# Attention and channel MLP on one core: from coarse phases ordered by a scheduler to one written order of even steps

## The chip, the cores and the metric

The kernel runs on one core of one Trainium2 chip, as a single launch. Times are device microseconds (us) of whole executions. The kernel before took 446.32 us at the median of three runs (440.49 to 447.17). The experiments came in four sets, each on another chip, with runs of the kernel before in each. The record calls a run slow when it took over 1.5% longer than the fastest run of the same kernel in its set; ratios leave slow runs out, the medians given here do not.

The engines have the profile's names: PE (matrix engine; PEld is its weight load), DVE (vector engine), ACT (scalar engine), POOL and SP. POOL and SP also issue DMAs. PEclk is the clock granted to PE, as a share of full speed. PSUM is the memory into which PE writes its results; a ring is a set of buffers used in turn. The span is the time from the first to the last instruction of an execution.

## The reference, cut to what matters

```python
# attention: q, k, v of (8 batches, 8 heads, 576 tokens, 64), omega (128, 64)
def phi(x):
    proj = np.einsum('bhsd,md->bhsm', x, omega)
    return np.concatenate([np.cos(proj), np.sin(proj)], axis=-1) / np.sqrt(m)
q_p, k_p = (phi(q), phi(k))
kv = np.einsum('bhsm,bhsd->bhmd', k_p, v)
z = np.sum(k_p, axis=2)
num = np.einsum('bhsm,bhmd->bhsd', q_p, kv)
den = np.einsum('bhsm,bhm->bhs', q_p, z)
...                                    # attn = num / den; x = heads side by side
# mixer: x (8, 576, 512), U (576, 32), V (32, 576), w_ch1 (512, 2048), w_ch2 (2048, 512)
h = xt @ U @ V                         # xt: x with tokens last
u = x + h.transpose(0, 2, 1)
ch = np.maximum(u @ w_ch1, 0.0) @ w_ch2
return (u + ch).astype(np.float32)
```

Work comes in 32 pairs of heads, four pairs to a batch. Two pairs share one load of k, q and v (a "quad" of heads). When a batch's four pairs are done, its tokens are mixed (U and V), and then the two MLP layers, W1 with relu and W2, can run. One batch needs 64 matmuls of 512 columns for each layer, and the ninth token row ("tail") of two batches is done together.

## The kernel before

Comments with L numbers give the lines that the profile names. A pair's attention is a chain over four engines. PE makes projections (`pk`, `pt`, `pq`), DVE turns them into integer angles, ACT takes the sine, POOL shifts the same angles in place by a quarter turn, and ACT takes the sine again for the cosine:

```python
def sine(g, a):
    ang, ft = st[g]
    low = ...
    nc.scalar.activation(out=ft[:, 0, a, :], in_=low, func=ACT.Sin, scale=TO_RAD)      # L181
    nc.gpsimd.tensor_scalar(out=ang[:, a, :], in0=ang[:, a, :], scalar1=TURN / 4.0,
                            scalar2=1.0, op0=ALU.add, op1=ALU.mult)                      # L182
def cosine(g, a):
    ...
    nc.scalar.activation(out=ft[:, 1, a, :], in_=low, func=ACT.Sin, scale=TO_RAD)      # L188
```

`key_values` and `numerators` then use these features (`kv_ps`, `nd`), and DVE divides into `x`. POOL also issues the loads of k, q and v, and copies ("widens") v into tiles with a column of ones:

```python
def load(n, names):
    for name in names:
        raw[name, n] = rawp.tile([P, 2, NS * D], BF16, name=f"{name}raw")
        ordered(nc.gpsimd.dma_start(raw[name, n], quad(...)))                           # L146
def widen_v(n):
    ordered(nc.gpsimd.tensor_copy(vq[n % NV][:, :, 0:D], raw.pop(("v", n))...))         # L149
```

The MLP of one batch is four chunks, one for each step: eight tiles of W1, eight tiles of W1, two token tiles of W2, two token tiles of W2.

```python
def channel_in(b, fs):                       # hid has one buffer
    for f0 in fs[::2]:
        h_ps = psum.tile([P, 2, SM], F32, name="h_ps", tag="mm")
        for f in range(2):
            for ct in range(NCT):
                nc.tensor.matmul(h_ps[:, f, :], w1(ct, f0 + f), uT[:, :, ct, :], ...)   # L351
            nc.scalar.activation(out=hid[:, f0 + f, :], in_=h_ps[:, f, :], func=ACT.Relu)  # L353

for s in range(1, NG + 6):
    if s >= 6:
        b, mc = divmod(s - 6, 4)
        if b < B:
            mlp_chunk(b, mc)
    n = s // 2 + 1
    if s % 2 == 0 and 4 <= n < NG // 2:
        load(n, "kqv")
        transpose_quad(n)
        widen_v(n)                           # the v whose load was just issued
    if s < NG:
        angles(s)
    ...
    if s != 4:
        attend(s - 1)                        # key_values, numerators, and every fourth time the mix
```

The framework's scheduler then reorders the instructions of each engine, so the order that runs is not quite this one. PSUM has a ring of two double banks for attention and mixing ("at") and one for the MLP ("mm").

## Time and profile before

| | before |
|---|---|
| median time | 446.32 us |
| span of the profiled execution | 441.5 us |
| PE, ACT, DVE, POOL busy | 376.0, 227.7, 199.7, 133.3 us |
| two batches in the steady part (pair 15 to pair 23) | 103.5 us |

PE is busy for most of the span. These are lines of the page's parts 1 and 2 for the kernel before: busy us with the share of the span, then tenths of busy time and of the clock in 40 slices.

```profile
PE 376.0 (85%) x3675; PEld 191.3 (43%) x3675; DVE 199.7 (45%) x338; ACT 227.7 (52%) x280; POOL 133.3 (30%) x145
...
PE   3866886988899988988899988978899989979995
...
PEclk9968898999999998989999998998999999998999
```

Busy time overstates the work. The next lines are groups of the same kernel: count, busy us, mean ns of one; after the second bar, the engine's idle time before them and what ended it.

```profile
L351 PE MATMUL h_ps<-uT,W1b 128*128 128x512 bf16 x512 | 127.6, 391 | 25.5 <-ACT hid L353 23.7 <-ACT qT L166 0.9
L376 PE MATMUL ch_ps<-W2b,hid 128*128 128x512 bf16 x512 | 127.0, 392 | 3.9 <-DVE o L379 3.9
```

One such matmul shows 391 ns, but the ends are 216 ns apart at the median; near the end of the span, from 401.02 us on, 64 in a row took 13.89 us (217 ns each). From here on we measure lost PE time as spacings between matmul ends of more than 0.4 us. They add to 104.9 us in the kernel before; this overstates the loss, as each of the 132 spacings also contains the time of the matmul that ends it, 0.216 us at the median for 512 columns.

W1 matmuls wait 23.7 us for relu (`hid`), in the second field above. Why relu is late can be seen in the waits: engine and instruction, what it waited for, us in total, times, longest.

```profile
ACT hid L353 <- PE h_ps L351: 73.4, 62, 19.1
...
PE h_ps L351 <- ACT hid L353: 23.7, 22, 4.2
POOL vq_108 L149 <- DMA vraw<-in_v_dram: 18.9, 4, 7.5
...
POOL vq_112 L149 <- DMA vraw<-in_v_dram: 17.1, 3, 5.9
...
POOL vq_110 L149 <- DMA vraw<-in_v_dram: 9.0, 2, 5.7
...
POOL vq_114 L149 <- DMA vraw<-in_v_dram: 7.1, 1, 7.1
```

The four buffers of v make 52.1 us of waiting. One such place is in the timeline of the kernel before (start, us, engine, line, operation, and in brackets the idle time before it):

```profile
155.59 0.73 POOL L146 DMA_DIRECT2D vraw<-in_v_dram  x1
...
163.68 1.15 POOL L149 COPY vq_108<-vraw 128x1152 bf16<-128x1152 bf16 x1 [4.79 <-DMA vraw<-in_v_dram]
164.80 1.14 POOL L182 TENSOR_SCALAR ang<-ang 128x1152 int32<-128x1152 int32 x1
165.97 1.16 ACT L188 ACTIVATE ft<-ang 128x1152 bf16<-128x1152 int16 x1 [3.69 <-POOL ang L182]
167.04 1.06 ACT L353 ACTIVATE hid<-h_ps 128x512 bf16<-128x512 f32 x2
167.67 0.61 PE L351 MATMUL h_ps<-uT,W1b 128*128 128x512 bf16 x2 [3.19 <-ACT hid L353]
```

POOL waits for a load that it issued just before, and widens; then comes the angle shift, then ACT's cosine, then relu, then PE, which had a gap of 3.19 us. Of the W1 matmuls that follow, eight in a row are 410 to 428 ns apart instead of 216: half clock (the granted clock from 167.6 to 171.3 us is 0.57).

### The profile page before, as it was taken

Reading aid. Unit: us, or ns where it says so; the run is one execution under the profiler, and the core shown is the slowest. Engines: PE = TensorE matmul, PEld = TensorE weight load, DVE = VectorE, ACT = ScalarE, POOL = GpSimd, SP = SyncE. Lnnn points to the kernel's source line nnn. Section 1 sums busy time; section 2 is a strip of 40 time slices with the busy share of each in tenths; the row PEclk is TensorE's granted clock in tenths of the full one; section 3 lists DMA queues with packets and bytes.
Section 4 is the critical chain, followed back from the end, with each engine's and each line's share of the span. In section 5 each row is a group of like instructions: output and inputs, shape, how many; then the busy total and the mean of one; then the engine's idle time right before and its main releaser. Section 6 shows DMA issues by size and latency. Waiting matters only on the chain.

```text
span 441.5 us, 8568 instructions
## 1 busy us (share of the span) xinstructions
PE 376.0 (85%) x3675; PEld 191.3 (43%) x3675; DVE 199.7 (45%) x338; ACT 227.7 (52%) x280; POOL 133.3 (30%) x145
## 2 busy tenths in 40 slices
PE   3866886988899988988899988978899989979995
PEld 2553343434464433434456443434446444434452
DVE  2966451564436541664435551674343462460011
ACT  2975684327834465625755094635773277504420
POOL 5794435313323240523333052433332121200000
PEclk9968898999999998989999998998999999998999
DMA  8999294858073590585536473285809320133023
GB/s 137 173 152 199 46 176 70 137 114 144 16 123 61 119 135 1 94 150 99 83 48 136 90 117 49 30 157 108 134 3 181 73 49 0 25 62 70 1 48 72
DMA packets 71765, 40.64 MB, mean 92 GB/s; under 512 B 50608, under 2 KB 66992, under 8 KB 71728
## 3 DMA queue, kind: packets, MB, share of 16 engines
q0 software_dynamic: 17280, 18.35, 27.5%
q1 hardware_dynamic: 54448, 21.75, 24.9%
q8 instruction: 28, 0.46, 0.5%
q14 instruction: 9, 0.07, 0.1%
HBM read 37.14 MB, written 9.44 MB: 105 GB/s over the span
## 4 chain that ended last, share of the span: by engine, by line
PE 48%; ACT 13%; DMA 11%; POOL 10%; DVE 9%; issue 8%; POOLq 0%; ACTq 0%; DVEq 0%
PE ch_ps L376 23%; PE h_ps L351 11%; DMA vraw<-in_v_dram 8%; POOL ang L182 5%; ACT ft L181 5%; DVE ang L172 5%; ACT ft L188 4%; DMA qraw<-in_q_dram 4%; PE ch_ps L388 3%; PE ht_ps L364 3%; ACT hid L353 3%; PE nd L266 2%; DVE u L325 2%; ACT hidt L366 1%; POOL kraw L146 1%
## 5 line engine op out<-in xcount | busy, mean ns | idle before, releaser
L351 PE MATMUL h_ps<-uT,W1b 128*128 128x512 bf16 x512 | 127.6, 391 | 25.5 <-ACT hid L353 23.7
L376 PE MATMUL ch_ps<-W2b,hid 128*128 128x512 bf16 x512 | 127.0, 392 | 3.9 <-DVE o L379 3.9
L182 POOL TENSOR_SCALAR ang<-ang 128x1152 int32<-128x1152 int32 x64 | 73.5, 1149 | 177.0 <-ACT ft L181 176.4
L353 ACT ACTIVATE hid<-h_ps 128x512 bf16<-128x512 f32 x128 | 73.2, 592 | 73.6 <-PE h_ps L351 73.4
L188 ACT ACTIVATE ft<-ang 128x1152 bf16<-128x1152 int16 x64 | 74.0, 1159 | 46.0 <-POOL ang L182 45.5
L181 ACT ACTIVATE ft<-ang 128x1152 bf16<-128x1152 int16 x64 | 73.9, 1160 | 39.4 <-DVE ang L172 36.5
L351 PEld LDWEIGHTS <-W1b 128*128 128x128 bf16 x512 | 48.2, 99 | 78.3 <-issue 32.6
L376 PEld LDWEIGHTS <-hid 128*128 128x128 bf16 x512 | 48.0, 100 | 61.2 <-issue 14.0
L379 DVE TENSOR_TENSOR o<-ch_ps,u 128x512 f32<-128x512 f32 x32 | 22.1, 690 | 85.2 <-PE ch_ps L376 84.9
L172 DVE TENSOR_SCALAR ang<-pk 128x1024 int32<-128x1024 f32 x32 | 39.0, 1220 | 39.9 <-PE pt L211 34.8
L172 DVE TENSOR_SCALAR ang<-pq 128x1024 int32<-128x1024 f32 x32 | 39.1, 1221 | 21.9 <-PE pq L221 21.7
L244 PEld LDWEIGHTS <-ft 64*128 64x128 bf16 x1152 | 24.0, 99 | 13.1 <-issue 7.4
L266 PEld LDWEIGHTS <-ft 128*128 128x128 bf16 x512 | 21.5, 101 | 16.4 <-issue 7.6
L266 PE MATMUL nd<-kvb,ft 128*128 128x65 bf16 x512 | 22.9, 198 | 6.1 <-DVE kvb L247 6.1
L247 DVE CAST kvb<-kv_ps 128x260 bf16<-128x260 f32 x32 | 13.5, 423 | 26.3 <-PE kv_ps L244 26.3
L366 ACT ACTIVATE hidt<-ht_ps 128x512 bf16<-128x512 f32 x16 | 9.5, 592 | 28.0 <-PE ht_ps L364 28.0
L279 DVE TENSOR_TENSOR x<-nd,rec 128x512 bf16<-128x512 f32 x32 | 22.1, 691 | 1.0
L325 DVE TENSOR_TENSOR u<-hn,x 128x1024 bf16<-128x1024 f32 x16 | 18.9, 1219 | 7.4 <-PE hn L324 7.4
L277 DVE RECIPROCAL nd<-nd 128x10 f32<-128x10 f32 x32 | 7.3, 228 | 28.0 <-PE nd L272 27.9
L364 PE MATMUL ht_ps<-utT,W1b 128*128 128x128 bf16 x256 | 16.9, 219 | 3.5 <-ACT hidt L366 3.5
L172 DVE TENSOR_SCALAR ang<-pt 128x256 int32<-128x256 f32 (+1 forms) x33 | 13.5, 408 | 12.8 <-PE pt L211 12.4
L364 PEld LDWEIGHTS <-W1b 128*128 128x128 bf16 x256 | 15.6, 98 | 6.1 <-issue 3.5
(70 smaller groups left out, 270.1 us busy)
## 6 DMA issues: line engine op xcount, KB each, us to landing
out_dram<-o SPq DMA_DIRECT2D x72, 128.0 KB, 2.4
kraw<-in_k_dram POOLq DMA_DIRECT2D x16, 288.0 KB, 4.4
qraw<-in_q_dram POOLq DMA_DIRECT2D x16, 288.0 KB, 6.3
vraw<-in_v_dram POOLq DMA_DIRECT2D x16, 288.0 KB, 7.1
W1b<-in_moe_w_ch_dram POOLq DMA_DIRECT2D x4, 512.0 KB, 8.4
W2b<-in_moe_w_ch_dram POOLq DMA_DIRECT2D x4, 512.0 KB, 9.6
Vf<-in_moe_V_dram SPq DMA_DIRECT2D x4, 72.0 KB, 2.3
kT<-kraw SPq DMA_TRANSPOSE x13, 4.5
```

The lines of the kernel that those rows point to most:

```text
L172: nc.vector.tensor_scalar(out=dst, in0=src, scalar1=TO_UNITS, scalar2=None, op0=ALU.mult)
L181: nc.scalar.activation(out=ft[:, 0, a, :], in_=low, func=ACT.Sin, scale=TO_RAD)
L182: nc.gpsimd.tensor_scalar(out=ang[:, a, :], in0=ang[:, a, :], scalar1=TURN / 4.0, scalar2=1.0, op0=ALU.add, op1=ALU.mult)
L188: nc.scalar.activation(out=ft[:, 1, a, :], in_=low, func=ACT.Sin, scale=TO_RAD)
L244: nc.tensor.matmul(kv_ps[:, hh, o], ft[r, f, 0, c:c + M], vq[n % NV][r, NS * i + s, :], start=(s == 0), stop=(s == NS - 1))
L266: nc.tensor.matmul(nd[:, t // 2, 2 * (t % 2) + hh, :], ft[:, f, 1, c:c + P], kvb[:, hh, f, :], start=(f == 0), stop=(f == 1))
L279: nc.vector.tensor_tensor(out=x[:, :, hp * P:(hp + 1) * P].rearrange("p (a t) (h d) -> p a t h d", a=2, h=2), in0=nd[:, :, 0:4, 0:D], in1= ...
L325: nc.vector.tensor_tensor(out=u[:, 2 * a:2 * a + 2, :], in0=h_ps, in1=x[:, 2 * a:2 * a + 2, :], op=ALU.add)
L351: nc.tensor.matmul(h_ps[:, f, :], w1(ct, f0 + f), uT[:, :, ct, :], start=(ct == 0), stop=(ct == NCT - 1))
L353: nc.scalar.activation(out=hid[:, f0 + f, :], in_=h_ps[:, f, :], func=ACT.Relu)
L364: nc.tensor.matmul(h_ps[:, a, f, :], w1(ct, f0 + 4 * a + f), utT[:, ct, :], start=(ct == 0), stop=(ct == NCT - 1))
L376: nc.tensor.matmul(ch_ps, hid[:, f, t * P:(t + 1) * P], W2b[:, f, :], start=(f == 0), stop=(f == NFT - 1))
```

## The change

Its intent: one order, written by hand, for all engines. Each of 38 steps holds one pair's attention, four W1 tiles of one batch, and one W2 token tile of the batch ahead of it, alternated inside the step. The hidden layer gets two buffers so that two batches overlap. Batch 0 is mixed by pairs in an opening of its own. A last loop pins each engine's instructions to the written order. Six of the eight loads of the weights are spread over steps 5 to 8, and v is widened one quad later. In PSUM, the MLP's ring becomes one double bank, mostly for W1, and two single banks, mostly for W2. The diff, cut to its core and condensed in places (cuts are marked by dots):

```diff
-    hidp = ctx.enter_context(tc.tile_pool(name="hidp", bufs=1))
+    hidp = ctx.enter_context(tc.tile_pool(name="hidp", bufs=2))
...
+        if tag == "h":          # two W1 tiles, one relu of 1024 columns, one PSUM buffer
+            nc.scalar.activation(out=hid[:, 2 * i:2 * i + 2, :], in_=h_ps, func=ACT.Relu)
...
+    def in_groups(s):           # W1: two groups of two tiles a step
+        if 5 <= s <= 8:
+            return [(0, 2 * (s - 5) + i) for i in range(2)]
+        b, j = divmod(s - 7, 4)
+        return [(b, 2 * j + i) for i in range(2)] if 1 <= b < B else []
+    def out_parts(s):           # W2: one token tile a step, in three parts
+        ...                     # batch 0: steps 9 to 14
+        b, t = divmod(s - 11, 4)
+        return [(b, t, r) for r in (range(0, 6), range(6, 11), range(11, 16))] if 1 <= b < B else []
+    def step(s):
+        loads(s)
+        if s < NG:
+            angles_k(s); angles_tail(s); sine(s, 0)
+        first(0)                               # W1
+        if s < NG:
+            angles_q(s); sine(s, 1)
+        if mb is not None: mix_in(mb)          # every fourth step
+        second(0)                              # W2
+        if s <= NG: key_values(s - 1)
+        if s < NG:  cosine(s, 0)
+        first(1)
+        if s < NG:  cosine(s, 1)
+        ...
+        second(1)
+        if s <= NG: numerators(s - 1)
+        ...
+        second(2)
+    def loads(s):
+        ...
+        elif s % 2 == 0 and n < NG // 2:
+            load(n, "kqv")
+            transpose_dma(n)
+            widen_v(n - 1)
...
-    for s in range(1, NG + 6):
-        ...
+    ...                                        # the opening: pairs 0 to 4, batch 0 mixed by pairs
+    for s in range(5, NG + 11):
+        step(s)
+    last = {}
+    for i in nc.cur_bb.bb.instructions:
+        if i.engine in last:
+            tc.add_manual_dep(i, last[i.engine], NOSYNC)
+        last[i.engine] = i.name
```

## The prediction

> **What bounds the kernel now.** The matrix engine (PE), through its stalls. The page shows PE busy 376.0 of 441.5 us, ACT 227.7, DVE 199.7, POOL 133.3. Busy is not work: end to end, the 512-column matmuls of the MLP follow each other at 216 ns (median in the trace) (391 ns each by the groups). [...] Each matmul group's median spacing times its count adds to about 333 us; about 105 us lies in spacings over 0.4 us. Of these, 35.6 end with ACT's relu `hid` (L353), 22.6 are mostly runs of 427 ns, matmuls at half clock after a stall (PEclk 0.8 in such slices), 9 end with kvb, 15 with u and o. Two batches take 103.6 us in the steady part (118.3 to 221.9), for 81 us of PE work.
>
> Why relu is late: in the waits, POOL waits 52 us for `vraw` from DMA before the widening copy; the chain has `vraw` at 8% of the span. Timeline, 155.6 to 167.7: POOL issues v's load, is held 4.8 us by the widening of that same load, widens, then shifts the angle; ACT's cosine stands behind it, relu behind the cosine, and PE has a 3.2 us gap, then matmuls at 427 ns. [...]
>
> The opening is the other loss: batch 0's mix is done near 36 us, yet the first W1 matmul is at 45, behind transposes of the fourth quad.
>
> **What the change does.** It widens v one load later; W1 tiles, W2 tiles and attention alternate in each step, with relu between sines; the hidden layer gets two buffers; relu mostly becomes one 1024-wide instruction (estimate 1.05 us for two at 0.59); the opening does only pairs 0 to 4 and mixes batch 0 by pairs. PE's work stays.
>
> **Estimate.** Opening: twenty sine passes of 1.05 to 1.16 us from 10.7 us plus copies, 88% dense: step 5 starts near 41 us. Steps 5 to 14 hold less PE work and are paced by ACT (4.65 us of sines plus 2.1 of relu) and DVE: 84 us. The 17 full steps: 6.9 us of MLP on PE, 2.75 of attention with switches, 1.3 for tails and mixing, 0.5 of waits (nd evacuation, relu before the second W1 tile): 11.4 each, 196 us, against 12.9 now. From step 32 nearly pure MLP: 77 us. Last eviction and store 4.5. Sum 403 of span; times run 2 us over: **405 us**, range 386 to 428. Faster by over 2%: 0.93; same 0.05; slower 0.02.
>
> **What would show it.** POOL's waits for vraw nearly gone; PE spacings over 0.4 us down from 105 to under 60 us; waits on hid under 15; steady PEclk without dips; two batches in about 91 us; first W1 matmul near 43 us; relu count nearly halved, ACT busy about 8 us lower.
>
> **What would make it wrong.** [...] If the single W1 buffer makes PE wait for relu behind a sine each step, or DVE's mix (4 us in one step of four) pushes the angles late, steps cost 12 to 13 us and the gain halves. If the clock drops in the ACT-paced steps 5 to 14, the ramp costs 10 more. Late loads would keep the opening at 45.

41, 84, 196, 77 and 4.5 make the 403 us of span, and 2 us more the 405. The terms are estimates. The order meant under "Why relu is late" is what the trace of the kernel before shows: the sine of q ended at 161.62 us, but its angle shift started only at 164.80, behind the widening (163.68, 1.15 us long); and two relus whose W1 matmuls had ended by 164.32 us started only at 167.04 and 167.52, behind the cosine (165.97, 1.16 us long). The "switches" of the estimate can be seen there too: a W1 matmul right after one of L244 ends 322 ns after it (median of 22), where W1 matmuls in a row are 216 ns apart.

## The result, and the profile after

| | before | after |
|---|---|---|
| median of the runs of the first set | 443.94 us (440.49 to 447.17, 4 runs) | 411.96 us (411.08 to 416.44, 4 runs) |
| ratio | | 0.9325, 95% interval 0.9228 to 0.9422 |
| span profiled | 441.5 us | 414.7 us |
| PE spacings over 0.4 us | 104.9 us | 67.9 us |
| two batches, pair 15 to 23 | 103.5 us | 89.2 us |

A ratio here is the mean time of one kernel's fast runs over that of the other's fast runs of the same rounds, so it is not the ratio of the medians quoted, which contain slow runs where there were any. The changed kernel ran twice more as the base of later sets: 412.4 us (ratio 0.9397) and 411.77 us (0.9304). The kernel before moved between sets, with medians from 437.4 to 443.9 us.

The same lines of the page, for the changed kernel:

```profile
PE 364.6 (88%) x3662; PEld 187.4 (45%) x3662; DVE 198.4 (48%) x338; ACT 217.7 (52%) x220; POOL 135.4 (33%) x146
...
PE   3367876577999899989999999899999999999995
...
PEclk9986998588899999999999999999999999999999
```

In the steady part, from slice 11 on, PE is at eight or nine tenths until the last slice, and its clock does not drop (in the repeat it drops once there, by one tenth in one slice, and the two batches take 90.7 us). The loss has moved to the left: slices 7 to 10, with 6, 5, 7 and 7 tenths, were 6, 9, 8 and 8 before. The groups say that PE hardly waits for relu any more (0.3 us against 23.7); the last line is the wide relu, 60 of twice the width beside 8 that stay narrow, in place of 128:

```profile
L383 PE MATMUL ch_ps<-W2b,hid 128*128 128x512 bf16 x512 | 128.0, 387 | 0.0
L355 PE MATMUL h_ps<-uT,W1b 128*128 128x512 bf16 x480 | 116.3, 386 | 0.3 <-ACT hid L359 0.3
L359 ACT ACTIVATE hid<-h_ps 128x1024 bf16<-128x1024 f32 x60 | 61.0, 1016 | 47.2 <-PE h_ps L355 46.4
```

POOL's waits for v are down from 52.1 to 7.6 us, and a new wait stands beside them in the waits of the changed kernel:

```profile
PE pt L200 <- DMA qT<-qraw: 8.8, 2, 6.4
...
POOL vq_103 L140 <- DMA vraw<-in_v_dram: 5.3, 2, 4.1
...
POOL vq_106 L140 <- DMA vraw<-in_v_dram: 2.3, 1, 2.3
```

The window view for two batches of the steady part, from pair 15's first matmul to pair 23's. First the kernel before (164.3 to 267.8 us), then the changed one (146.8 to 236.0 us): length, busy us of each engine with its instructions, granted clock, DMA share, GB/s.

```profile
164.30:267.80 103.50, 90.83 (x901) 45.06 (x900) 48.75 (x82) 55.57 (x68) 32.22 (x34) 0.97 0.54 94
```

```profile
146.80:236.00 89.20, 86.12 (x904) 43.35 (x904) 48.60 (x81) 53.35 (x53) 31.48 (x32) 1.00 0.65 107
```

Pair by pair, the trace shows how unevenly attention went before. The starts of successive pairs in the kernel before are 5.2, 11.0, 16.4, 13.5, 11.6, 9.3, 18.0 and 18.6 us apart (pairs 13 to 21). In the changed kernel eight such steps (pairs 14 to 22) take 8.8, 9.8, 9.7, 12.2, 13.9, 10.2, 10.2 and 12.0 us.

These starts also show where the time was gained. Pair 15 starts 17.5 us earlier than before (146.8 against 164.3 us), but by then only 192 of the 1,024 matmuls of 512 columns of W1 and W2 (tails left out) are done, against 296; the 104 put off are worth 22.5 us at 216 ns. From pair 15 to 31 both kernels do 512 of them, in 177.8 against 205.9 us: 28.1 us gained. From pair 31 to the end the changed kernel needs 18.8 us more (90.1 against 71.3), as the work put off comes there. So the gain of 26.8 us in these two profiles comes from the steady part; opening and ramp are not better for their work than before.

The stages add up as follows in the changed kernel, beside the terms of the prediction. "Pair n" is the start of its first matmul in the trace.

| stage | predicted, us | measured, us | from the trace |
|---|---|---|---|
| opening, to step 5 | 41 | 44.9 | pair 5 starts at 44.9 |
| steps 5 to 14 | 84 | 101.9 | pair 15 starts at 146.8 |
| 17 full steps | 196 | 188.9 | pair 31 at 324.6: 11.11 a step, times 17 |
| from step 32 | 77 | 75.1 | last output tile ready at 410.8 |
| end | 4.5 | 3.9 | span 414.7 |

The repeat of the changed kernel in the second set has 47.8 us for the opening and 93.9 us for the ramp of steps 5 to 14, so the ramp varies between executions. The 6.4 us wait for `qT` is there in the first profile, and not in the repeat:

```profile
70.54 0.21 PE L198 MATMUL pt<-WT,kT 64*128 64x128 bf16 x1 [0.64 <-DVE u L301]
...
77.16 0.26 PE L200 MATMUL pt<-qT,WT 64*128 64x128 bf16 x1 [6.41 <-DMA qT<-qraw]
...
77.98 1.16 ACT L170 ACTIVATE ft<-ang 128x1152 bf16<-128x1152 int16 x1 [8.17 <-DVE ang L161]
```

### The profile page after: what moved, and what is told of

The parts are those of the page before. It is cut to its first block, busy times and chain, and to the rows that moved or that the text cites. A ratio compares the mean times of both kernels' runs of the same rounds, so it can differ in the third digit from the quotient of the medians.

```text
span 414.7 us, 8470 instructions
## 1 busy us (share of the span) xinstructions
PE 364.6 (88%) x3662; PEld 187.4 (45%) x3662; DVE 198.4 (48%) x338; ACT 217.7 (52%) x220; POOL 135.4 (33%) x146
## 4 chain that ended last, share of the span: by engine, by line
PE 74%; DVE 12%; DMA 8%; issue 2%; ACT 2%; POOL 1%; SPq 0%; DVEq 0%; ACTq 0%; POOLq 0%
PE h_ps L355 26%; PE ch_ps L383 25%; DMA qT<-qraw 7%; PE kv_ps L229 4%; PE nd L251 3%; PE ch_ps L399 3%; DVE x L267 3%; DVE ang L161 3%; PE pq L210 2%; PE ht_ps L371 2%; DVE u L301 2%; DMA kraw<-in_k_dram 2%; DVE nd L262 1%; DVE ut L311 1%; PE nd L257 1%
## 5 line engine op out<-in xcount | busy, mean ns | idle before, releaser
L355 PE MATMUL h_ps<-uT,W1b 128*128 128x512 bf16 x480 | 116.3, 386 | 0.3 <-ACT hid L359 0.3
L359 ACT ACTIVATE hid<-h_ps 128x1024 bf16<-128x1024 f32 x60 | 61.0, 1016 | 47.2 <-PE h_ps L355 46.4
L355 PEld LDWEIGHTS <-W1b 128*128 128x128 bf16 x512 | 46.5, 99 | 60.9 <-issue 9.8
L386 DVE TENSOR_TENSOR o<-ch_ps,u 128x512 f32<-128x512 f32 x32 | 21.9, 685 | 53.4 <-PE ch_ps L383 53.4
L301 DVE TENSOR_TENSOR u<-hn,x 128x1024 bf16<-128x1024 f32 x16 | 19.5, 1218 | 12.4 <-PE hn L300 12.3
L189 PE MATMUL pk<-WT,kT 64*128 64x128 bf16 x256 | 13.8, 231 | 9.9 <-DVE x L267 3.6
L267 DVE TENSOR_TENSOR x<-nd,rec 128x512 bf16<-128x512 f32 x32 | 21.8, 682 | 0.2
L189 PEld LDWEIGHTS <-kT 64*128 64x128 bf16 x256 | 8.5, 99 | 19.7 <-issue 10.5
L210 PE MATMUL pq<-qT,WT 64*128 64x512 bf16 x64 | 13.9, 427 | 3.9 <-DVE ang L161 3.9
```

What stands on the lines that cost most here:

```text
L189: nc.tensor.matmul(pk[:, e, j * P:(j + 1) * P], kT[r, c, :], WT[r, :])
L267: nc.vector.tensor_tensor(out=x[:, :, hp * P:(hp + 1) * P].rearrange("p (a t) (h d) -> p a t h d", a=2, h=2), in0=nd[:, :, 0:4, 0:D], in1= ...
L301: nc.vector.tensor_tensor(out=u[:, 2 * a:2 * a + 2, :], in0=h_ps, in1=x[:, 2 * a:2 * a + 2, :], op=ALU.add)
L355: nc.tensor.matmul(h_f, w1(ct, 2 * i + f), uT[:, :, ct, :], start=(ct == 0), stop=(ct == NCT - 1))
L359: nc.scalar.activation(out=hid[:, 2 * i:2 * i + 2, :], in_=h_ps, func=ACT.Relu)
```

## The experiments

Three questions were open. First: was the held POOL queue, as predicted, what the gain came from, or was it the order? The theory A of the prediction is that a wait for v's load delays relu; the rival B is that the even mixture of work does the good and hides such waits. Second: which part of the order matters? Third: why is the ramp 10 to 18 us longer than estimated?

All kernels gave correct results. Short names: e1 is v widened at once, e2 v widened later in the kernel before, e3 the order not pinned, e4 k and q earlier, e5 blocks, e6 phases, e7 relu cut in two, and e8, e10 and e11 the three runs with angles written ahead. In the profiles of e1, e3, e4 and e11 some matmul records are missing (3,608 of 3,662 are there), and in that of e2 too (3,643 of 3,675), which makes false wide spacings, so for these we use starts of pairs and waits, and no sum of spacings but one. The first set (e1 to e4) had no run of the changed kernel in it, so these are compared with it across sets. The record's own verdict for these four and for e6 is "unclear"; three of the seven runs of the kernel before were slow in the first set.

### v widened at once in the changed kernel

```diff
             load(n, "kqv")
             transpose_dma(n)
-            widen_v(n - 1)
+            if s == 10:
+                widen_v(5)
+            widen_v(n)
```

> The changed kernel, but from step 10 on each quad's v is widened right after its own load is issued, as the kernel before does. Theory A (a load that holds POOL's queue was the main cause of the late relus): POOL waits 40 us or more for vraw again, the steady step goes from 11.1 us back towards 12.5 to 13, and the time to 430 to 445 us. Rival B (the even mixture of work within each step carries the gain and hides such a hold): within 5 us of the changed kernel's 412.

Measured: 414.88 us (412.21 to 416.72), beside a kernel before of 437.38 us; ratio 0.9532 (0.9443 to 0.9621). POOL's waits for v are back, as this line of its waits shows:

```profile
POOL vq L140 <- DMA vraw<-in_v_dram: 46.5, 9, 6.5
```

But the two batches from pair 15 to 23 take 90.9 us, as in the repeat of the changed kernel (90.7 us), and PE waits for relu for 1.6 us in all:

```profile
145.40:236.30 90.90, 86.45 (x888) 43.67 (x904) 48.63 (x82) 53.48 (x53) 31.29 (x32) 0.98 0.63 105
```

One of POOL's waits in its timeline:

```profile
180.10 1.16 ACT L170 ACTIVATE ft<-ang 128x1152 bf16<-128x1152 int16 x1 [5.55 <-DVE ang L161]
180.33 1.14 POOL L140 COPY vq<-vraw 128x1152 bf16<-128x1152 bf16 x1 [6.32 <-DMA vraw<-in_v_dram]
...
181.45 1.14 POOL L171 TENSOR_SCALAR ang<-ang 128x1152 int32<-128x1152 int32 x1
```

POOL is held for 6.32 us, but the sine that its next angle shift must wait for ends only at 181.26, and the shift starts at 181.45. With one pair in about 11 us, POOL reaches its loads long before it is needed (here it waits from 174.01 us on, 7.25 us before that sine ends). So 46.5 us of waiting cost at most a few us: rival B is right for the changed kernel as pinned, and A is wrong there. The total of 414.9 is within 3 us of 412; its ratio is a little worse than those of the changed kernel in other sets, so a small cost, of up to about 2%, is not ruled out.

### v widened later in the kernel before

```diff
             load(n, "kqv")
             transpose_quad(n)
-            widen_v(n)
+            if n > 4:
+                widen_v(n - 1)
+        if s % 2 == 0 and n == NG // 2:
+            widen_v(n - 1)
```

> The kernel before, but with v widened two steps after its load. Theory A: POOL's 52 us of waits for vraw go under 15, PE spacings over 0.4 us that end with relu fall from 35.6 to under 18, and the time falls from 444 to 420 to 432 us. Rival B: relu still comes late because of the coarse phases; 439 to 446 us.

Measured: 422.66 us (421.44 to 424.18) against 437.38 us; ratio 0.9717 (0.9642 to 0.9793). POOL waits for v only 3.5 us, and this line of the waits, 23.7 us before, is halved:

```profile
PE h_ps L351 <- ACT hid L353: 12.6, 20, 0.9
```

The medians differ by 14.7 us, but that of the kernel before contains three slow runs; by the fast runs the edit takes off about 12 us. So in the kernel before, theory A was right in part. One expectation failed: the spacings that end with relu fell from 35.6 to 24.7 us, not under 18 (missing records make this sum uncertain, but the line above, 12.6 of 23.7 us, says much the same). By both counts more than half of relu's lateness in the kernel before has another cause than v's load. Together the two runs say that the two causes overlap. The late widening alone is worth 2.8%, and the whole change 6 to 7%; inside the pinned order it is worth little or nothing, because that order already covers the wait. Here two batches take 97.9 us from pair 15 to 23 (granted clock 0.98), still 7 to 9 us more than the changed kernel:

```profile
155.70:253.60 97.90, 88.79 (x893) 44.76 (x900) 48.80 (x82) 55.53 (x69) 31.48 (x32) 0.98 0.58 98
```

### The written order not pinned

```diff
         if i.engine in last:
-            tc.add_manual_dep(i, last[i.engine], NOSYNC)
+            pass
```

> The changed kernel without its last loop, so that the scheduler may reorder what the program writes. If the pinned order itself carries the gain: 425 us or more. If the way it is written (steps, buffers, loads) carries it: 408 to 416 us.

Measured: 420.21 us (418.09 to 422.27); ratio 0.9659 (0.9571 to 0.9747). This is between the two cases expected: about 8 us over the changed kernel. The steady part isn't slower (87.5 us for two batches), so the pin isn't needed there: the way it is written is enough. Pair 15 starts at 153.9 us instead of 141.7 to 146.8. Most of that is lost in the opening (pair 5 starts at 53.2 us instead of 44.9 to 47.8), where the scheduler put pair 2's first matmul where it waited 10.5 us for the transposed k. In the ramp, a W1 matmul at 89 us waited 12.7 us, and its timeline shows the chain of theory A again:

```profile
84.91 1.15 POOL L140 COPY vq<-vraw 128x1152 bf16<-128x1152 bf16 x1 [8.18 <-DMA vraw<-in_v_dram]
86.03 1.15 POOL L171 TENSOR_SCALAR ang<-ang 128x1152 int32<-128x1152 int32 x1
87.21 1.16 ACT L177 ACTIVATE ft<-ang 128x1152 bf16<-128x1152 int16 x1 [15.57 <-POOL ang L171]
88.28 0.58 ACT L357 ACTIVATE hid<-h_f 128x512 bf16<-128x512 f32 x1
88.91 0.59 PE L355 MATMUL h_f<-uT,W1b 128*128 128x512 bf16 x1 [12.67 <-ACT hid L357]
```

A wait for v's load holds POOL, the angle shift, ACT's cosine, relu and then PE. So what e1 shows, that such a wait is harmless, holds for the steady part of the pinned order and not for every order of the same program.

### The attention of a step as one block

```diff
-        first(0)
         if s < NG:
             angles_q(s)
             sine(s, 1)
 ...
-        first(1)
-        if s < NG:
             cosine(s, 1)
 ...
         if s <= NG:
             numerators(s - 1)
+        first(0)
+        second(0)        # step 11: before first(0), as in the changed kernel
+        second(1)
+        first(1)
```

> The changed kernel, with each step's attention written as one block and its MLP tiles after it as another; the amount of each step stays. If the alternation inside the step carries the gain over the kernel before: relu stands behind all four sine passes, PE waits for it once a step, the steady step goes from 11.1 to 12.5 us or more, 430 us or more. If only the even amount of work per step matters: under 418 us.

Measured: 484.96 us (481.75 to 486.05), ratio 1.102 (1.0954 to 1.1086): slower than either kernel by far. The steady step takes 14.40 us. So the alternation inside a step matters most of all parts tested. But the expected mechanism was wrong: PE does not wait for relu (its waits list none of PE's matmuls for `hid`). It waits for DVE at each turn of the attention chain (`pq` for angles 35.2 us, 29 times; `nd` for kvb 20.1 us, 23 times), since nothing is written between its links:

```profile
156.04 0.41 DVE L161 TENSOR_SCALAR ang<-pt 128x256 int32<-128x256 f32 x1
156.18 0.39 PE L210 MATMUL pq<-qT,WT 64*128 64x512 bf16 x2 [1.28 <-DVE ang L161]
...
157.75 0.42 DVE L232 CAST kvb<-kv_ps 128x260 bf16<-128x260 f32 x1
...
158.22 0.67 PE L251 MATMUL nd<-kvb,ft 128*128 128x65 bf16 x16 [0.96 <-DVE kvb L232]
```

Spacings over 0.4 us that end with angles add to 53.4 us and those with kvb to 24.9 us, and the granted clock falls to 0.911. In two batches it is 0.90:

```profile
154.40:268.80 114.40, 95.39 (x904) 49.81 (x902) 47.84 (x80) 55.95 (x54) 31.47 (x32) 0.90 0.50 82
```

### The old phases in the new order

Each batch again has two steps with eight W1 tiles and two with two W2 token tiles each, but alternated with attention inside the step, and pinned.

```diff
-        return [(b, 2 * j + i) for i in range(2)] if 1 <= b < B else []
+        return [(b, 4 * j + i) for i in range(4)] if 1 <= b < B and j < 2 else []
 ...
-        b, t = divmod(s - 11, 4)
+        b, j = divmod(s - 7, 4)
+        ...              # j of 2 and 3: token tiles 2 * (j - 2) and the next, of the same batch
 ...
-    for s in range(5, NG + 11):
+    for s in range(5, NG + 7):
```

> The changed kernel with the old phases: two steps of four with eight W1 tiles, two with two W2 token tiles each, alternated with attention inside the step and pinned. If the even share of W1 and W2 per step carries the gain: the W1 steps are paced by ACT (4.65 us of sines and 4.1 of relu) and DVE, four steps cost 47 us or more against 44.4, 422 us or more. If the fine alternation is enough: 404 to 414 us, as it also ends two steps earlier and fills the ramp.

Measured: 432.36 us (430.15 to 433.3), ratio 0.9827 (0.9762 to 0.9893), 20 us over the changed kernel. Two batches take 95.6 us:

```profile
163.60:259.20 95.60, 87.57 (x903) 44.37 (x904) 49.37 (x81) 53.26 (x60) 31.48 (x32) 0.98 0.61 100
```

So even shares are worth some 5 to 6 us in two batches, about 12 us of the 20 over the 17 full steps, if it is the phases. Outside them the edit does two opposite things: the ramp from pair 5 to 15 takes 117.6 us instead of 93.9 in the repeat, and the stretch from pair 31 to the end 75.4 instead of 90.1, as the program has four steps less. But again the mechanism expected was wrong. The W1 steps are the fast ones, 9.3 us each, and not paced by ACT as expected (the waits of this run list none of PE's matmuls for `hid`). The W2 steps take 12.4 to 18.5 us: pq waits 0.9 to 1.3 us for the angles there, since a W2 step has no MLP tile written in that place, and the tail's W1 tiles, which this edit put into one step, wait three times 0.69 us for their relu (`hidt`). That last part is the edit's own doing, so the size of the effect of phases alone is not settled.

### Relu cut in two

```diff
-            nc.scalar.activation(out=hid[:, 2 * i:2 * i + 2, :], in_=h_ps, func=ACT.Relu)
+            for f in range(2):
+                nc.scalar.activation(out=hid[:, 2 * i + f, :], in_=h_ps[:, f, :], func=ACT.Relu)
```

> The changed kernel with each 1024-wide relu cut into two of 512, as before: ACT gets 60 more passes, near 10 us more busy time. If ACT has slack in the new order: within 3 us of the changed kernel's 412. If relu's end still sets when the second W1 tile may start: 417 us or more.

Measured: 413.03 us (407.37 to 417.62) beside 411.77 us for the changed kernel in the same set; ratios 0.9346 (0.923 to 0.9462) and 0.9304 (0.9197 to 0.9411). Half of the runs of both were slow; the fast ones have means of 409.9 and 408.0 us. The wide relu is worth nothing that can be measured here, which fits an ACT with slack; the intervals are wide, so a per cent either way is not ruled out.

### The base of the second and the third set

> The changed kernel itself, as the base for this set: 409 to 414 us, steady step 11.1 us. It also tells whether the widening at once (414.9 us in the set before) costs anything: if this is 411 or more beside a kernel before of about 437, the widening at once cost under 4 us in the new order.

> The changed kernel, as the base for this set: 410 to 414 us.

Measured: 412.4 us and 411.77 us, as in the first set.

### k and q loaded earlier in the ramp

The wait for `qT` at 71 to 77 us belongs to quad 4. The transposes of quads 4 and 5 by DMA run beside the loads of W1 and W2; the slowest qT took 20.0 us from issue to landing in the first profile of the changed kernel, and the median one 4.0 us.

```diff
     load(3, "kq")
+    load(4, "kq")
 ...
-            load(4, "kq")        # step 5
+            load(5, "kq")
 ...
-            load(5, "kq")        # step 7
```

> The changed kernel with the k and q loads of quads 4 and 5 issued one place earlier, so that their transposes do not run beside the loads of W1 and W2. Theory: the 6.4 us wait for qT at 71 to 77 us and about 2 us of half clock after it go, 404 to 409 us. Rival: the opening is held by the chain of PE and DVE, the wait was covered or moves to another load: 410 to 414 us.

Measured: 408.34 us (406.93 to 411.11), ratio 0.9376 (0.929 to 0.9462). The median lies in the range expected, but the ratio is no better than the changed kernel's 0.9304 to 0.9397, so a gain isn't shown. The slowest qT took 8.8 us, PE waited for qT for at most 3.1 us, and that in the opening, and the ramp took 93.9 us, exactly as in the repeat of the changed kernel, which had no long wait either. So this edit does not shorten a ramp that has no long wait; whether it makes the long wait rarer is not shown by one profile. Half clock remains: from 47.24 us eight W1 matmuls took 3.58 us in this profile, where eight from 51.65 us took 1.90.

### The next pair's angles written ahead, in the ramp

In the ramp PE waited for DVE: spacings over 0.4 us that end with `x`, `u`, `ut` and angles add to 15.4 us from pair 5 to 15 in the changed kernel. Attention has two PSUM buffers, and pt of the next pair can only start when the numerators in the buffer are divided (the waits of the changed kernel have pt at L198 waiting for `x` for 2.4 us, 6 times). The edit writes the next pair's first angles before this step's numerators, in steps 5 to 13, on top of the earlier loads:

```diff
+        def front(g):
+            angles_k(g); angles_tail(g); sine(g, 0)
+        def early(g):
+            return 6 <= g <= 14
         loads(s)
-        if s < NG:
-            angles_k(s); angles_tail(s); sine(s, 0)
+        if s < NG and not early(s):
+            front(s)
 ...
         second(1)
+        if early(s + 1):
+            front(s + 1)
         if s <= NG:
             numerators(s - 1)
```

> The kernel with early k and q loads (408.3 us in the set before), and in steps 5 to 13 the next pair's first angles are written before this step's numerators. If the ramp is paced by the turn of PE and DVE over the two attention buffers in PSUM (numerators, their eviction, then the next pair's pt): the ramp from pair 5 to pair 15 shrinks from 94 us by 8 to 15, 394 to 401 us. If it is paced by DMA or by the half clock: 405 us or more.

Measured: 420.35 us (416.92 to 425.46), ratio 0.9536 (0.9465 to 0.9607): slower than the changed kernel. Pairs 5 to 11 did go faster, 45.9 us against 55.6 us in the repeat of the changed kernel. Then a new wait stood in the way, shown in its timeline and in the view of the tile uT:

```profile
100.87 3.57 PE L355 MATMUL h_ps<-uT,W1b 128*128 128x512 bf16 x8 [6.07 <-DMA uT<-u]
```

```profile
DMA to landing us min/median/max: 4.2/5.8/14.2
```

POOL ran ahead and issued the three loads of quad 6 at 86.1 to 87.6 us, just when SP issued the transpose of batch 1's u at 86.66 us. It landed 14.2 us later.

### The same, with two loads written later

```diff
-        loads(s)
+        if s not in (10, 14):
+            loads(s)
 ...
             sine(s, 1)
+        if s in (10, 14):
+            loads(s)
```

> The kernel with the next pair's angles written ahead in the ramp (420 us in the set before), and with the loads of steps 10 and 14 written after the second sine pass, so that they are issued after the transposes of u and not beside them. If the 11.8 us that PE waited for uT there came from loads sharing the DMA engines with the transpose (14 us from issue to landing against 4.8): uT lands about 5 us after its issue, and the time falls to 399 to 407 us. If the transpose is slow for another reason: 415 us or more.

Measured: 411.3 us (408.61 to 411.77), ratio 0.9366 (0.9298 to 0.9435). That the loads caused the new wait is confirmed, with one reservation: the transposes of quad 6's k and q follow its loads, so they moved with them. No transpose of u took more than 5.9 us, batch 1's took 4.3 us, and PE no longer waits for uT:

```profile
DMA to landing us min/median/max: 4.2/4.7/5.9
```

But the time is only that of the changed kernel, a miss. The ramp takes 92.8 us: pairs 11 to 15 now take 10.4, 9.8, 11.1 and 12.5 us apiece instead of 8.8 to 11.8 us, as nd waits 0.5 to 1.5 us in each step for the angles written before it. The order gained where steps hold little MLP work, and gave it back where they hold more.

### Written ahead only where it gained

```diff
-            return 6 <= g <= 14
+            return 6 <= g <= 10
 ...
-        if s not in (10, 14):
+        if s != 10:
```

> As the run before it (411.3 us), but the next pair's angles are written ahead only up to pair 10, where they gained (pair 5 to 11: 49 us against 52 to 60 without), and no longer for pairs 11 to 14, where the steps became longer (10 to 12.5 us against 8.8 and 8.9); only step 10's loads are later. If the losses there came from the new order: the ramp from pair 5 to 15 takes 86 to 89 us, the time 402 to 407 us, 1 to 2% under the changed kernel's 412. If the ramp is bound by something that merely moves: 409 to 413 us.

Measured: 404.44 us (403.11 to 409.75, 6 runs), ratio 0.9157 (0.9122 to 0.9192). The ramp from pair 5 to 15 takes 85.9 us, just under the 86 to 89 expected. This version beats the kernel before, and by all that is on record the changed one: its interval lies just below those of the changed kernel's three sets (the lowest begins at 0.9197), but it was not run in one set with it, and the two sets with its repeats were on other chips. The profile agrees: only the ramp is shorter than in the repeat of the changed kernel (by 8.0 us), the opening (48.0 us) and the steady part (90.7 us) are not. The page of this kernel:

```profile
PE   3456787779998999899999999899999999999995
...
PEclk9995999999999999899999999999999999999999
```

Slices 6 to 10, which were 7, 6, 5, 7 and 7 tenths in the changed kernel, are now 8, 7, 7, 7 and 9, and the clock drops less.

## Why the prediction was right or wrong

- **The time** was predicted as 405 us with a range of 386 to 428, and it is 412. The direction, the range and the chance for "faster" were right. That the sum came so close is in part luck: in the first profile opening and ramp took 21.8 us more than predicted, and the other three terms 9.6 us less.
- **What bounds the kernel** was right. The gain is in PE's spacings over 0.4 us (104.9 to 67.9 us; under 60 was predicted, a miss) and in two batches of the steady part (89.2 us; 91 was predicted). Waits on `hid` went from 35.6 to 0.7 us, counted as spacings, and POOL's for v to 7.6 us.
- **Why relu is late** was right in part as a description of the kernel before: there, the late widening alone gives about 12 us, but 24.7 of the 35.6 us of spacings that end with relu stay. As an account of what the change gains, it was wrong. In the new order 46.5 us of the same wait return and the steady part does not change. The prediction named one wait; the run with blocks shows that the new order rests on alternation inside the step, and the run with phases, less cleanly, that even steps help.
- **The full steps** were right: 11.4 us predicted, 11.11 measured (11.21 in the repeat). The term for waits was right too: from pair 15 to 31 the spacings over 0.4 us, less 0.216 us each for the matmul itself, add to 5.2 us, 0.3 us a step against the 0.5 predicted. In the kernel before they add to 33.2 us, so their fall makes up the whole gain of the steady part.
- **The ramp** is the term that was mis-sized. The prediction has "Steps 5 to 14 hold less PE work and are paced by ACT (4.65 us of sines plus 2.1 of relu) and DVE: 84 us." They took 101.9 us in the first profile and 93.9 in the repeat. ACT did not pace them: from 47 to 147 us it was busy for 62.4 of 100 us. The step that failed was to take an engine's busy time for the pace of a stage in which that engine is one link of a chain. With little MLP work written between the links, PE waited for DVE's evictions (15.4 us in the first profile), for a transpose beside the weights' loads (6.7 us), and ran partly at half clock. The shorter ramp of the last experiment, 85.9 us with the same amount of work, shows that 8 us of it is an effect of order, as the ramp with early k and q alone took 93.9.
- **The clock** was named as a danger ("If the clock drops in the ACT-paced steps 5 to 14, the ramp costs 10 more"), and it did drop: the profile has runs of W1 and W2 matmuls at 427 ns at 62 to 65, 78 to 81, 90 to 92 and 101 to 106 us, 22 such spacings, which at 211 ns each cost about 5 us. The drop at 62 us did not follow one long wait: from 58 to 63 us PE was idle for no more than 1.12 us at a time, but from 59 to 62 us it was busy for only half of the time. These are two windows of 3 us in the changed kernel (length, PE busy first, the granted clock third from the end); what makes the clock drop is not shown by them:

```profile
59.00:62.00 3.00, 1.53 (x15) 0.83 (x16) 3.00 (x4) 2.87 (x4) 3.00 (x5) 1.00 1.30 115
62.00:65.00 3.00, 3.00 (x41) 1.42 (x41) 0.96 (x2) 2.19 (x2) 1.79 (x2) 0.51 1.43 163
```

- **The opening** was 4 us longer than predicted, and the first W1 matmul came at 45.8 us, not near 43; in the kernel before it came at 44.4, so nothing was gained there. The chain through the mix of batch 0 leaves ACT idle from 31.1 to 36.2 us; no run tried to shorten it.
- **The wide relu** lowered ACT's busy time by 10.0 us (8 predicted), but it is worth nothing in time, as the run with relu cut in two shows.
- **Left open**: what the second buffer of `hid` is worth by itself. With one buffer the written order could not run, as relu would have to write the next batch's first tile before PE has read this batch's last one; this is argued from the code, not tried. The new split of PSUM and the new opening were not varied by themselves either.

## What to carry to other kernels

In these runs the waits of an engine with slack were harmless or costly depending on the pace of the work around them. POOL's waits for v, 52.1 us in all, cost about 12 us when work came in bursts, and 46.5 us of them cost nothing that the steady part shows when each step had the same mixture. So write independent work between the links of a chain (this was worth more than 70 us here), share work evenly over steps, and only then look at single waits. Estimate a stage with little filler work by its chain of evictions, not by its busiest engine, and look at which transfers a faster order will push against each other (here the transpose of u took 14.2 us from issue to landing beside three loads, and 4.3 us when they came later).
